# Loading keys and queries of two batches as 128 long runs instead of 96-row pieces

## The chip, the cores and the metric

The kernel runs on one core of a Trainium2 chip. Its time is the device time of one execution in microseconds (us). A core has a matrix engine (TensorE, in the profile PE for its matmuls and PEld for its weight loads), a vector engine (VectorE, DVE), a scalar engine (ScalarE, ACT), GpSimd (POOL) and SyncE (SP), which here does nothing but issue the DMAs of the kernel, one after the other, in one queue. Sixteen DMA engines carry them out.

## The reference

Everything is float32. With q, k, v of shape [8 batches, 8 heads, 576 tokens, 64] and p of [8, 8, 32, 64]:

```python
p_packed = sm_attn(p, k, v)                # 32 packed rows attend to the 576 tokens
out = sm_attn(q, p_packed, p_packed)       # each token attends to the 32 packed rows
x = out.transpose(0, 2, 1, 3).reshape(4608, 512)
h = x @ w_in;  x = (h * sigmoid(h)) @ w_out          # 512 -> 2048 -> 512
h = x @ w_in2; return (h * cos(h)) @ w_out2          # 512 -> 2048 -> 512
```

Here sm_attn(q, k, v) is softmax(q k^T / 8) v. The weights come in as 64-bit words and are decoded to float32 on the core.

## The kernel before

**Phases.** The long part is two stretches of dense matmuls: `first` (lines 985 to 1042) is the first MLP, in 16 steps of 128 hidden columns for each stretch of tokens, and `second` (1211) is the second MLP, in blocks of 256 positions. Ahead of `first` lies the attention. Batches 0 and 1 are done at the very start by the class `Boot` (line 755); batches 2 to 7 are done beside `first` by the class `Steady`, which loads in another way and isn't touched here.

**The order of the work.** Nothing is emitted in program order. Every instruction is recorded in a plan (`Plan`, line 80) with a price in ns (`price`, 163) and what it depends on; a list scheduler (`schedule`, 310) with due times (`DUE`, 469) simulates the engines and the DMA queue by these prices, several times from both ends, and the order that comes out of it is the static order of each engine's instructions and of SP's queue. A DMA's price is its bytes by a rate in GB/s (line 193). A copy may go to ACT or DVE, as the scheduler sees fit (`copy`, 573). Where the plan leaves PE idle between 6 and 60 us, the kernel puts small matmuls on the identity there (`busy`, 1246, called at 429), whose results nobody reads.

**Batches 0 and 1.** `Boot.load` (770) brings a tensor of one batch into one tile `bx` (three of them: k, v, q) by four DMAs of two heads each: 96 partitions, each with a run of six tokens of 64 numbers (1536 bytes) for each head. So partition r holds the tokens 6r to 6r+5 of every head. `turned` (785) transposes pairs of tokens, [96 x 128] to [128 x 96], three for a head, into a PSUM bank, and copies the 288 columns to a tile `bkt`: the even tokens of a pair in the lower 64 partitions, the odd ones in the upper. It does this for the four heads of one group g (0 or 1) at a time, into two of four `bkt` tiles that k and q share.

`stage1` (823) is the attention of p to k: `scores` (806) from `bkt` and the transposed p (`pbd`), the maxima and a copy of the scores to `ba` (834), exponentials, transposes of `ba` in six chunks of 96 (to `bat`). `weighted` (854) multiplies by v: chunk c of the scores must hold the tokens that lie at one place of v's six in all 96 partitions (`values`, 800). Its result is `ppf`. `products` (934) multiplies `ppf` by the first weights. `stage2` (887) turns q, takes the scores against `ppf`, and makes the softmax in the tile `a2`, which `first` reads. Batch 1 uses the same tiles as batch 0, so its loads wait until batch 0 has read them; `change` at line 1307 gives the room of all `Boot` tiles to later weights, once both batches are done.

**Order of tokens.** The columns of `a2` for batches 0 and 1 are not in the order of tokens but as the transposes left them, and stay so through both MLPs. `output` (1135) undoes it: each piece of a block's 128 result rows that lies in one run of 96 positions is written by one DMA, with a step of 6 rows in the output (1143 to 1150). For the other batches the step is 1.

Of the kernel before, what the change touches and what calls it, by code (L numbers as in the profile page):

```python
# [12 lines left out]
F32 = mybir.dt.float32  # L13
F32R = mybir.dt.float32r
I32 = mybir.dt.int32
# [64 lines left out]
class Plan:  # L80
# [4 lines left out]
    PE, DVE, ACT, POOL, DMA, NONE = "PE", "DVE", "ACT", "POOL", "DMA", "NONE"  # L85
# [77 lines left out]
    def price(self, engine, f, out, ins):  # L163

        n = math.prod(out.shape[1:])
        m = max([math.prod(x.shape[1:]) for x in ins], default=n)
        sbuf = all(not str(x.space).endswith("PSUM") for x in ins)
        strided = 44 if ins and n >= 96 and ins[0].ap[-1][0] == 2 else 110 if n >= 96 and out.ap[-1][0] > 2 else 0
        if engine == self.PE:
            if f == "transpose":  # L170
                return 3 + n / 1.2, 0

            if ins[0].dtype == F32R:
                return n / 2.4 + (18 if n == 512 else 7 if n == 256 else 13), 0
            rows, k = out.shape[0], ins[0].shape[0]
            if rows == 128:
                return n * 3.33 + 10, 0
            if rows == 64:
                return n * 0.82, 0
            return {64: 30 if k == 96 else 37, 288: 65, 512: 117}[n], 0  # L180
        if engine == self.DVE:
            if f == "transpose":
                return (67 if sbuf else 160) + (100 if n == 128 else 0) + n / 0.92, 0
            fast = sbuf and f in ("tensor_copy", "tensor_scalar", "memset") and m == n
            if f == "scalar_tensor_tensor" and sbuf and ins[0].dtype == F32:
                return 67 + n / 0.53, 0
            return 67 + max(max(m, n) / (1.92 if fast else 0.96), 60 if f == "reciprocal" else 0) + strided, 0
        if engine == self.ACT:
            return (94 if sbuf else 51) + max(m, n) / 1.2 + (190 if f == "accumulate" else 0) + (105 if f == "sin" else 0) + strided, 0
        if engine == self.POOL:  # L190
            return 149 + (1.7 if any(0 in [st for st, _ in x.ap] for x in ins) else 2.1) * n, 0
        run = min(map(self.contiguous, (out, *ins)))
        return self.ISSUE, 4 * math.prod(out.shape) / (232 if out.dtype == I32 else 260 if run >= 128 else 150)

    @staticmethod
    def contiguous(x):
# [239 lines left out]
def attention_mlps_kernel(  # L436
# [13 lines left out]
    B, H, S, D = q.shape  # L450
# [3 lines left out]
    P = 128  # L454
    HALF = S // 2
# [11 lines left out]
    plan = Plan(nc)  # L467
# [4 lines left out]
    V, A, T, G, DMA = plan.V, plan.A, plan.T, plan.G, plan.D  # L472
# [16 lines left out]
    bpool = boot_stack.enter_context(pool("boot", "right"))  # L489
# [10 lines left out]
    def tiles(pl, shape, dtype, name, n):  # L500

        ts = [pl.tile(shape, dtype, name=f"{name}{i}") for i in range(n)]
        cells.setdefault(pl, []).extend(t.tensor.name for t in ts)
        return ts


    def place(g, h2):
        return (g + h2) % 2
# [14 lines left out]
    STEP = 64  # L523
# [19 lines left out]
    rows = {s: flat(f"m{s}", WIDTH) for s in (1, 2)}  # L543
# [18 lines left out]
    ident = const.tile([P, P], F32, name="ident")  # L562
# [10 lines left out]
    def copy(dst, src):  # L573
        with plan.either():
            A.copy(dst, src)
            V.tensor_copy(dst, src)
# [119 lines left out]
    def cut(t, shape):  # L696
        t = t[:, : math.prod(shape[1:])]
        return t if len(shape) == 2 else t.rearrange("p (a b) -> p a b", a=shape[1])

    CH = 96  # L700
    NCH = S // CH

    class Steady:

        @staticmethod
        def spot(h2, hf):
            return 64 * (h2 ^ hf), HALF * hf

        def __init__(self):
            self.kins = ring(tiles(att, [P, NB, 32], F32, "kin", 2))  # L710
            self.vins = ring(tiles(att, [P, 4 * len(self.chunks), D], F32, "vin", 2))
            self.bigs = ring(tiles(att, [P, S], F32, "big", 3))
            self.a1ts = ring(tiles(att, [P, len(self.chunks) * P], F32, "a1t", 2))
# [41 lines left out]
    class Boot:  # L755

        @staticmethod
        def spot(h2, hf):
            return 64 * hf, HALF * h2

        chunks = [slice(c, c + CH) for c in range(0, S, CH)]

        def __init__(self):
            self.x = dict(zip("kvq", tiles(bpool, [P, H, NCH, D], F32, "bx", 3)))
            self.kt = tiles(bpool, [P, S], F32, "bkt", 4)
            self.a = tiles(bpool, [P, S], F32, "ba", 2)
            self.at = tiles(bpool, [P, NCH * P], F32, "bat", 2)
            self.pp = tiles(bpool, [P, P], F32, "bpp", 2)

        def load(self, n, src, b):  # L770
            plan.unit = ("load", n, b)
            for g in range(2):
                for j in range(2):
                    h = slice(4 * g + 2 * j, 4 * g + 2 * j + 2)
                    DMA.dma_start(
                        self.x[n][:CH, h].rearrange("r h c d -> r h (c d)"),
                        src[b, h].rearrange("h (r c) d -> r h (c d)", c=NCH),
                    )

        def get(self, name, shape, g, j=0):  # L780
            if name == "a1":
                return self.a[g]
            return cut({"kt": self.kt[2 * g + j], "s": self.a[g], "pp": self.pp[g]}.get(name, self.at[g]), shape)

        def turned(self, src, b, g, bank):
            x = self.x["k" if src is k else "q"]
            ts = []
            for j in range(2):
                t = self.get("kt", [P, S], g, j)
                for h2 in range(2):  # L790
                    st = bank()
                    with plan.together():
                        for m in range(3):
                            pair = x[:CH, 4 * g + 2 * j + h2, 2 * m : 2 * m + 2, :].rearrange("r c d -> r (c d)")
                            T.transpose(st[:, m * CH : (m + 1) * CH], pair, ident[:CH, :CH])
                    copy(t[:, h2 * HALF : (h2 + 1) * HALF], st[:, :HALF])
                ts.append(t)
            return ts

        def values(self, b, g):  # L800
            return lambda c, h2, j: self.x["v"][:CH, 4 * g + 2 * j + h2, 2 * (c % 3) + c // 3, :]

    ppf = {}
    a2 = {}
# [18 lines left out]
    def stage1(b, g, bank, mem):  # L823
        plan.unit = ("stage1", b, g)

        plan.margin = plan.SPARE if b >= 2 else 0
        chunks = mem.chunks
        kt = mem.turned(k, b, g, bank)
        a1 = mem.get("a1", [P, S], g)
        mx = maxes()  # L830
        sts = scores(g, pbds[b % 2][:, 2 * g : 2 * g + 2], lambda h2: h2, kt, bank, mem.spot)
        for hf, st in enumerate(sts):
            V.tensor_reduce(mx[:, hf : hf + 1], st, axis=AX.X, op=ALU.max)
            copy(a1[:, hf * HALF : (hf + 1) * HALF], st)
        m = ms()
        V.tensor_scalar(m, mx[:, 0:1], mx[:, 1:2], -SCALE, op0=ALU.max, op1=ALU.mult)
        sums = sumss()
        A.activation(a1[:, :S], a1[:, :S], AF.Exp, bias=m, scale=SCALE, accum_out=sums)
        rs = rss()
        V.tensor_scalar(rs, sums, 1e-9, None, op0=ALU.add)  # L840
        V.reciprocal(rs, rs)
        n = len(chunks)
        lens = [len(range(S)[c]) for c in chunks]
        a1t = mem.get("a1t", [P, n, P], g)
        for c0, c1 in ((0, 4), (4, n)):
            st = bank()
            r = lens[c0]
            for c in range(c0, c1):
                T.transpose(st[:r, (c - c0) * P : (c - c0 + 1) * P], a1[:, chunks[c]], ident)
            copy(a1t[:r, c0:c1, :], st[:r, : (c1 - c0) * P].rearrange("p (c n) -> p c n", n=P))  # L850
        plan.margin = 0
        return lens, a1t, mem.values(b, g), rs
# [282 lines left out]
    def output(i, t):  # L1135

        o = oring()
        if t % 2:
            V.tensor_scalar(o, acc[t], WEIGHT**-2, None, op0=ALU.mult)
        else:  # L1140
            A.activation(o, acc[t], AF.Copy, scale=WEIGHT**-2)
        p0 = order[i] * TB + t % 2 * P
        cuts = [p0] + [c for c in range(p0 + 1, p0 + P) if c % (CH if c <= S else HALF) == 0] + [p0 + P]
        for a, b in zip(cuts, cuts[1:]):
            n, m = divmod(a, HALF)
            if n < 2:
                r0, step = n * S + m % CH * NCH + m // CH * 2 + t // 2, NCH
            else:
                r0, step = n * S + t // 2 * HALF + m, 1
            DMA.dma_start(out[r0 : r0 + (b - a - 1) * step + 1 : step, :], o[a - p0 : b - p0])  # L1150

    gt, st, m5s = {}, {}, {}

# [241 lines left out]
```

## Time and profile before

| | |
|---|---|
| time, median of 3 runs | 1477.23 us (1475.91 to 1480.18) |
| the profiled execution's own time | 1478.51 us |
| its span | 1476.7 us |
| instructions | 34030 |
| ACT busy | 761.9 us (52%) |
| bytes moved by DMA | 296.52 MB, 201 GB/s over the span |

The span is the time from the first to the last instruction that the profile has; some 1.8 us lie around it. Busy time of an engine is the sum of its instructions; matmuls are pipelined, so a busy PE may still be a PE that runs short of its best. The identity matmuls that fill gaps count as busy too.

### The profile page before, as it was taken

The numbers are of one execution on the slowest core, as the hardware profiler recorded it, in microseconds if no ns is written. First come the engines' busy times: TensorE is split into PE (matmuls) and PEld (weight loads), VectorE is DVE, ScalarE is ACT, GpSimd is POOL, SyncE is SP. The second block draws the span as 40 slices with busy tenths as digits, with TensorE's granted clock in tenths as the row PEclk, the third lists the DMA queues.
The fourth block names the chain that finished last, engine by engine and source line by source line (L and its number), as shares of the span: only waits on it lengthen the run. The fifth ranks groups of instructions, "written<-read, shape, count | busy, mean of one in ns | idle before, by whom it ended". The sixth has DMA issues, their size and how long they took to land.

```text
span 1476.7 us, 34030 instructions
## 1 busy us (share of the span) xinstructions
PE 1465.8 (99%) x13100; PEld 1402.8 (95%) x13100; DVE 1139.9 (77%) x2344; ACT 761.9 (52%) x1571; POOL 0.7 (0%) x6
## 2 busy tenths in 40 slices
PE   8999999999999999999999999999999999999998
PEld 6899888899899998999999999999999999999998
DVE  6998787767887687866487778888787877777765
ACT  6976554545456455555354444454454544444443
POOL 0000000000000000000000000000000000000000
PEclk9999999999999999999999999999999999999999
DMA  9776665876867656354777758777676657575560
GB/s 272 210 243 187 163 169 128 242 206 153 215 178 205 208 150 192 129 188 167 268 263 227 228 185 255 230 237 237 214 222 201 215 180 240 182 233 184 191 197 36
DMA packets 313985, 296.52 MB, mean 201 GB/s; under 512 B 172512, under 2 KB 218080, under 8 KB 313824
## 3 DMA queue, kind: packets, MB, share of 16 engines
q1 hardware_dynamic: 313824, 294.35, 66.1%
q8 instruction: 103, 1.69, 0.5%
q14 instruction: 58, 0.48, 0.1%
HBM read 242.81 MB, written 51.45 MB: 199 GB/s over the span
## 4 chain that ended last, share of the span: by engine, by line
PE 96%; DVE 2%; ACT 1%; DMA 0%; issue 0%; SPq 0%; DVEq 0%; ACTq 0%
PE acc L213 54%; PE hb L213 24%; PE mb L213 9%; PE sb L213 9%; DVE rsb L213 0%; ACT ba L213 0%; DMA bx<-in_k 0%; DMA kin<-in_k 0%; DVE ba L213 0%; DVE big L213 0%; ACT bkt L213 0%; DVE wy L213 0%; DVE mx L213 0%; DVE r L213 0%; DVE a L213 0%
## 5 line engine op out<-in xcount | busy, mean ns | idle before, releaser
L213 PE MATMUL acc<-g,w 128*128 128x256 f32 (+2 forms) x3072 | 470.1, 295 | 0.0
L213 PEld LDWEIGHTS acc<-g,w 128*128 128x128 f32 x3072 | 424.7, 188 | 23.4 <-issue 20.5
L213 PE MATMUL acc<-w,g 128*128 128x256 f32 x3456 | 426.7, 276 | 0.0
L213 PEld LDWEIGHTS acc<-w,g 128*128 128x128 f32 x3456 | 408.0, 188 | 0.0
L213 ACT ACTIVATE gf<-hb 128x320 f32<-128x320 f32 (+2 forms) x208 | 95.8, 467 | 103.7 <-PE hb L213 83.4
L213 ACT CAST g<-gf 128x320 fp32r<-128x320 f32 (+2 forms) x194 | 94.4, 488 | 106.1 <-PE acc L213 77.8
L213 DVE TENSOR_TENSOR g<-gf,g 128x320 fp32r<-128x320 f32 (+2 forms) x208 | 108.4, 523 | 46.0 <-PE acc L213 34.2
L213 DVE SCALAR_TENSOR_TENSOR gf<-gf,hb 128x320 f32<-128x320 f32 (+2 forms) x208 | 106.8, 518 | 45.6 <-ACT gf L213 44.4
L213 PE MATMUL hb<-a,w 128*128 128x320 f32 (+2 forms) x768 | 139.9, 298 | 0.6 <-DVE a L213 0.3
L213 PE MATMUL hb<-a,m 128*128 128x320 f32 (+2 forms) x768 | 129.0, 295 | 0.0
L213 ACT ACTIVATE r<-r,half_pi 128x512 f32<-128x512 f32 x144 | 103.7, 720 | 36.9 <-DVE r L213 36.8
L213 ACT CAST g<-r 128x512 fp32r<-128x512 f32 x144 | 89.6, 622 | 61.9 <-DVE r L213 61.7
L213 PEld LDWEIGHTS hb<-a,w 128*128 128x128 f32 x768 | 112.1, 188 | 9.8 <-issue 6.1
L213 PEld LDWEIGHTS hb<-a,m 128*128 128x128 f32 x768 | 109.5, 188 | 7.4 <-issue 5.7
L213 DVE TENSOR_TENSOR g<-r,g 128x512 fp32r<-128x512 f32 x144 | 99.3, 690 | 15.9 <-ACT g L213 15.6
L213 PE MATMUL hb<-w,m 128*128 128x256 f32 x768 | 110.8, 276 | 0.0
L213 DVE SCALAR_TENSOR_TENSOR r<-n,r 128x512 f32<-128x512 int32 x144 | 99.2, 689 | 2.2
L213 ACT ACTIVATE n<-hb 128x512 int32<-128x512 f32 x72 | 43.3, 602 | 108.4 <-PE hb L213 96.5
L213 PEld LDWEIGHTS hb<-w,m 128*128 128x128 f32 x768 | 97.9, 188 | 0.2 <-DVE mb L213 0.2
L213 DVE TENSOR_TENSOR hb<-hb,gf 128x256 f32<-128x256 f32 x72 | 31.1, 432 | 58.0 <-PE hb L213 58.0
L213 ACT ACTIVATE n<-mb 128x512 int32<-128x512 f32 x36 | 21.6, 601 | 82.2 <-PE mb L213 82.1
L213 DVE TENSOR_SCALAR r<-r 128x512 f32<-128x512 f32 x144 | 61.2, 425 | 2.6
(212 smaller groups left out, 1990.7 us busy)
## 6 DMA issues: line engine op xcount, KB each, us to landing
m<-w2s SPq DMA_DIRECT2D x504, 256.0 KB, 3.7
w<-w1dram SPq DMA_DIRECT2D x96, 256.0 KB, 3.7
w2s<-wd SPq DMA_DIRECT2D x28, 512.0 KB, 3.3
wd<-in_moe_w_in SPq DMA_DIRECT2D x24, 512.0 KB, 4.9
wd<-in_moe_w_out SPq DMA_DIRECT2D x20, 512.0 KB, 4.4
raw<-ydram SPq DMA_DIRECT2D x72, 128.0 KB, 3.9
w2dram<-wd SPq DMA_DIRECT2D x16, 512.0 KB, 3.0
w<-w2dram SPq DMA_DIRECT2D x16, 512.0 KB, 5.5
```

The source lines that it names most:

```text
L213: run = lambda: emit(*[real(x) for x in args], **{k: real(x) for k, x in kw.items()})
```

## The change

Keys and queries of batches 0 and 1 are loaded with all 128 partitions: partition 16h + r holds the tokens 36r to 36r + 35 of head h, 9216 bytes in one piece of DRAM, fetched by two DMAs of 4608 bytes for each partition. A transpose now turns two tokens of all eight heads at once, 18 of [128 x 128] for a tensor instead of 24 of [96 x 128]; they are done for both groups when group 0 is due, with five copies of up to 512 columns. k and q have a tile each for the turned form. v is loaded as before. Since v's order of tokens stays, the copy of the scores to `ba` puts them in v's order, with a step of six elements (`place`). The results of batches 0 and 1 are written in runs of 16 positions with a step of 36 rows.

The plan's rates change too: 300 instead of 232 GB/s for integer tiles, and 340 for runs of at least 1024 elements. The entry for 256 columns is a price for small float32 matmuls.

```diff
-            return {64: 30 if k == 96 else 37, 288: 65, 512: 117}[n], 0
+            return {256: 60, 64: 30 if k == 96 else 37, 288: 65, 512: 117}[n], 0
...
-        return self.ISSUE, 4 * math.prod(out.shape) / (232 if out.dtype == I32 else 260 if run >= 128 else 150)
+        return self.ISSUE, 4 * math.prod(out.shape) / (300 if out.dtype == I32 else 340 if run >= 1024 else 260 if run >= 128 else 150)
...
+        RUN = 16
+        STEP = S // RUN
...
-            self.x = dict(zip("kvq", tiles(bpool, [P, H, NCH, D], F32, "bx", 3)))
-            self.kt = tiles(bpool, [P, S], F32, "bkt", 4)
+            self.x = dict(zip("kq", tiles(bpool, [P, self.STEP, D], F32, "bx", 2)))
+            self.v = tiles(bpool, [P, H, NCH, D], F32, "bv", 1)[0]
+            self.kt = dict(zip("kq", tiles(bpool, [P, H, HALF], F32, "bkt", 2)))
...
+            rows = src[b].rearrange("h (r c) d -> (h r) (c d)", c=self.STEP)
+            for c0, c1 in ((0, self.STEP // 2), (self.STEP // 2, self.STEP)):
+                DMA.dma_start(self.x[n][:, c0:c1].rearrange("p c d -> p (c d)"), rows[:, c0 * D : c1 * D])
...
+            for m0 in range(0, self.STEP // 2, 4) if g == 0 else ():
+                m1 = min(m0 + 4, self.STEP // 2)
+                st = bank()
+                with plan.together():
+                    for m in range(m0, m1):
+                        T.transpose(st[:, (m - m0) * P : (m - m0 + 1) * P], self.x[n][:, 2 * m : 2 * m + 2].rearrange("p c d -> p (c d)"), ident)
+                copy(
+                    t[:, :, self.RUN * m0 : self.RUN * m1].rearrange("p h (m r) -> p m h r", r=self.RUN),
+                    st[:, : (m1 - m0) * P].rearrange("p (m h r) -> p m h r", m=m1 - m0, h=H),
+                )
+            return [t[:, 4 * g + 2 * j : 4 * g + 2 * j + 2].rearrange("p h n -> p (h n)") for j in range(2)]
+
+        def place(self, a, st):
+            copy(
+                a.rearrange("p (w r u) -> p u w r", w=NCH // 2, r=self.RUN),
+                st.rearrange("p (u w r) -> p u w r", w=NCH // 2, r=self.RUN),
+            )
...
-            copy(a1[:, hf * HALF : (hf + 1) * HALF], st)
+            mem.place(a1[:, hf * HALF : (hf + 1) * HALF], st)
...
-        cuts = [p0] + [c for c in range(p0 + 1, p0 + P) if c % (CH if c <= S else HALF) == 0] + [p0 + P]
+        run, step = boot.RUN, boot.STEP
+        cuts = [p0] + [c for c in range(p0 + 1, p0 + P) if c % (run if c <= S else HALF) == 0] + [p0 + P]
...
-                r0, step = n * S + m % CH * NCH + m // CH * 2 + t // 2, NCH
+                r0, by = n * S + m % run * step + m // run * 2 + t // 2, step
```

## Rows read from the trace of the kernel before

**Rows 1.** The page: busy us, share and count of engines.
```profile
PE 1465.8 (99%) x13100; PEld 1402.8 (95%) x13100; DVE 1139.9 (77%) x2344; ACT 761.9 (52%) x1571; POOL 0.7 (0%) x6
```

**Rows 2.** Busy time in stretches: stretch, length, busy (count) by engine, clock, DMA, GB/s.
```profile
5.00:10.00 5.00, 5.00 (x41) 4.39 (x39) 2.10 (x8) 2.55 (x7) 0.00 (x0) 1.00 1.04 337
10.00:15.00 5.00, 4.78 (x54) 3.67 (x47) 4.16 (x12) 4.41 (x12) 0.00 (x0) 1.00 1.05 322
15.00:20.00 5.00, 4.45 (x79) 4.16 (x79) 4.63 (x11) 2.82 (x6) 0.00 (x0) 1.00 1.09 270
20.00:25.00 5.00, 4.76 (x81) 3.38 (x81) 2.67 (x5) 2.87 (x7) 0.00 (x0) 1.00 1.08 286
25.00:30.00 5.00, 4.87 (x55) 2.88 (x53) 3.00 (x8) 3.44 (x10) 0.00 (x0) 1.00 1.06 275
...
100.00:120.00 20.00, 20.00 (x160) 18.98 (x159) 20.00 (x43) 15.65 (x37) 0.00 (x0) 1.00 0.76 237
```

**Rows 3.** The same view, the first 66 us in one stretch.
```profile
0.00:66.00 66.00, 59.43 (x705) 48.42 (x706) 52.33 (x142) 50.59 (x124) 0.70 (x6) 1.00 0.89 244
```

**Rows 4.** The chain that ended last, first 140 us: start, us, what.
```profile
0.73 3.14 DMA bx<-in_k
...
61.62 0.48 DVE ba L213
...
65.29 0.44 ACT a L213
...
94.50 5.66 PE acc L213 x43
```

**Rows 5.** Timeline: start, us, engine, line, operation, result<-operands, count, idle before.
```profile
4.01 1.19 PE L213 MATMUL acc<-ident,bx 96*128 96x96 f32 x6 [4.01 <-DMA bx<-in_k]
...
9.34 0.81 PE L213 MATMUL acc<-bkt,pbd 64*32 64x288 f32 x16
...
15.56 2.34 PE L1248 MATMUL acc<-ident 128*128 128x64 f32 x20
...
17.83 0.88 PE L213 MATMUL acc<-bx,bat 96*32 96x64 f32 x48
...
22.78 0.88 PE L213 MATMUL acc<-bx,bat 96*32 96x64 f32 x48
...
26.63 0.45 PE L213 MATMUL hb<-bkt,ppf 64*32 64x288 f32 x4
...
30.51 0.78 PE L213 MATMUL hb<-bkt,ppf 64*32 64x288 f32 x7
...
34.08 0.53 PE L213 MATMUL hb<-a,w 128*128 128x288 f32 x2
```

**Rows 6.** DMA packets between 18 and 22 us.
```profile
DMA packets 766, 1.11 MB, mean 276 GB/s; under 512 B 56, under 2 KB 765, under 8 KB 765
```

**Rows 7.** DMA packets between 8 and 10 us.
```profile
DMA packets 233, 0.83 MB, mean 416 GB/s; under 512 B 30, under 2 KB 30, under 8 KB 233
```

**Rows 8.** DMA issues of the first 60 us: count, KB each, median us to landing.
```profile
bx<-in_q SPq DMA_DIRECT2D x8, 288.0 KB, 11.0
```

**Rows 9.** Groups by form, first 66 us: count, busy us, mean ns, idle before.
```profile
L1248 PE MATMUL acc<-ident 128*128 128x64 f32 x106 | 14.2, 274 | 0.0
...
L213 ACT ACTIVATE wde<-wde 128x512 int32<-128x512 uint32 x11 | 7.6, 694 | 0.0
...
L213 ACT COPY bkt<-acc 128x288 f32<-128x288 f32 x12 | 4.8, 403 | 5.8 <-PE acc L213 5.5
...
L213 ACT COPY bat<-sb 96x512 f32<-96x512 f32 x2 | 1.2, 582 | 0.3 <-PE sb L213 0.2
...
L213 ACT COPY bat<-mb 96x256 f32<-96x256 f32 x2 | 0.7, 372 | 0.0
```

**Rows 10.** DMAs that write the output: issue ns (min/median/max), first and last start.
```profile
L213 SPq DMA_DIRECT2D out<-o x54: 332/413/1203, 824.1 to 1473.7; - x54
```

**Rows 11.** Waits of SP's queue after 700 us: total us, times, longest.
```profile
SPq L213 <- PE hb L213: 308.4, 177, 4.1
```

More of the change, by code (lines that the diff above doesn't have):

```diff
@@ L707, in spot, with place @@
             return 64 * (h2 ^ hf), HALF * hf
+        @staticmethod
+        def place(a, st):
+            copy(a, st)
         def __init__(self):
@@ L771, in load @@
             plan.unit = ("load", n, b)
-            for g in range(2):
-                for j in range(2):
-                    h = slice(4 * g + 2 * j, 4 * g + 2 * j + 2)
+            if n == "v":
+                for h in range(0, H, 2):
                     DMA.dma_start(
-                        self.x[n][:CH, h].rearrange("r h c d -> r h (c d)"),
-                        src[b, h].rearrange("h (r c) d -> r h (c d)", c=NCH),
-                    )
+                        self.v[:CH, h : h + 2].rearrange("r h c d -> r h (c d)"),
+                        src[b, h : h + 2].rearrange("h (r c) d -> r h (c d)", c=NCH),
+                    )
+                return
+            rows = src[b].rearrange("h (r c) d -> (h r) (c d)", c=self.STEP)
+            for c0, c1 in ((0, self.STEP // 2), (self.STEP // 2, self.STEP)):
+                DMA.dma_start(self.x[n][:, c0:c1].rearrange("p c d -> p (c d)"), rows[:, c0 * D : c1 * D])
         def get(self, name, shape, g, j=0):
@@ L782, in get @@
                 return self.a[g]
-            return cut({"kt": self.kt[2 * g + j], "s": self.a[g], "pp": self.pp[g]}.get(name, self.at[g]), shape)
+            return cut({"s": self.a[g], "pp": self.pp[g]}.get(name, self.at[g]), shape)
         def turned(self, src, b, g, bank):
[L786 to L798, printed above, removed]
+            n = "k" if src is k else "q"
+            t = self.kt[n]
+            for m0 in range(0, self.STEP // 2, 4) if g == 0 else ():
[14 more added lines that the diff above has]
+            )
         def values(self, b, g):
-            return lambda c, h2, j: self.x["v"][:CH, 4 * g + 2 * j + h2, 2 * (c % 3) + c // 3, :]
+            return lambda c, h2, j: self.v[:CH, 4 * g + 2 * j + h2, 2 * (c % 3) + c // 3, :]
     ppf = {}
@@ L1146, in output @@
             if n < 2:
-                r0, step = n * S + m % CH * NCH + m // CH * 2 + t // 2, NCH
+                r0, by = n * S + m % run * step + m // run * 2 + t // 2, step
             else:
-                r0, step = n * S + t // 2 * HALF + m, 1
-            DMA.dma_start(out[r0 : r0 + (b - a - 1) * step + 1 : step, :], o[a - p0 : b - p0])
+                r0, by = n * S + t // 2 * HALF + m, 1
+            DMA.dma_start(out[r0 : r0 + (b - a - 1) * by + 1 : by, :], o[a - p0 : b - p0])
     gt, st, m5s = {}, {}, {}
```

## The prediction

> **What bounds the kernel now.** I read the page first. PE is busy for 1465.8 of 1476.7 us [rows 1]: over the whole there is almost no idle time to win, so the question is where a busy PE does useless or thin work. The busy times by stretch answer it. Between 100 and 120 us PE gets through 160 matmuls in 20 us, one in 125 ns, without idle time [rows 2]; that is the dense state, and it lasts to the end. The first 66 us are different: PE counts as busy for 59.4 us [rows 3], but 14.2 us of that are 106 identity matmuls put into gaps [rows 9], and much else is small attention work. The change can pay only by bringing forward the moment from which PE is dense, or by thinning out what precedes it.
>
> The chain of waits shows that moment. It runs over PE, ACT and DVE pieces of batch 0 and 1, and the last part that isn't PE goes from 61.62 us (DVE, batch 1's second softmax) to the ACT cast of `a` that ends at 65.73; after it the chain stays on PE, as in the piece of 43 matmuls at 94.5 us [rows 4]. So I take 66 us as the end of the start-up, and what ends it is softmax and decoding on DVE and ACT, not a DMA.
>
> Two resources are short ahead of that. The DMA engines are full: their share is 1.04 to 1.09 in each 5 us stretch from 5 to 30 us [rows 2], and the issues of q take 11.0 us at the median to land, since they stand behind others [rows 8]. DVE has idle time only early: 2.90, 0.84, 0.37, 2.33 and 2.00 us in the five stretches from 5 to 30 us, 8.4 in all [rows 2]. Over 66 us it is busy for 52.3 [rows 3], and of the 13.7 idle us 8.4 are those and up to 5 lie in the first 5 us, so from 30 us on DVE is as good as full. Work that DVE gets earlier, in place of these 8.4 us, moves everything behind it.
>
> The timeline says what DVE waits for between 20 and 30 us. The second product with v runs at 22.78 us, the scores of q for group 0 at 26.63 and for group 1 at 30.51, the first matmul of the MLP at 34.08 [rows 5]. The scores need `ppf` and q. Twenty identity matmuls stand ahead of the first product with v, from 15.56 to 17.90 us [rows 5]: the plan expected to wait here.
>
> **The change part by part.**
>
> Transfers. One tensor of one batch has 8 x 576 x 64 x 4 = 1.18 MB. From 18 to 22 us nearly all packets lie between 512 bytes and 2 KB, which are the 1536-byte runs of k, q and v: 276 GB/s [rows 6], so 4.27 us for a tensor. From 8 to 10 us, 203 of 233 packets lie between 2 and 8 KB, the rows of the weights (512 KB on 128 partitions, so 4096 bytes): 416 GB/s [rows 7], so 2.84 us. In both stretches the engines are full, so this is the price by length. No row has a run of 4608 bytes; the nearest is 4096, and I take its rate: 1.43 us saved for each of four tensors. The low end is the rate of before, saving nothing; above 416 I don't go. What counts for batch 0 is when q has landed. Ahead of that lie its k, itself, and about half of batch 1's k, which the queue puts in between: 2.5 tensors, 3.6 us. k comes first of all, when little queues behind it and the first wait is mostly its own flight (issued at 0.73, first transposes at 4.01 [rows 4, 5]), so I count half of its part: 2.9 us, with ends 0 and 3.6.
>
> The Trainium skill has a rule against this term: its page "DMA: Bandwidth & Descriptors", section "Specifications", gives 512 bytes as the least transfer for line rate, so that runs of 1536 bytes would be at full rate already. The trace disagrees, 276 against 416 GB/s [rows 6, 7]; by the rule this term would be 0 and the sum 0.6 us.
>
> The first step. Transposes of group 0 now need a part of every head, and both halves of k instead of its first two DMAs. Against that the scores of group 0 run only at 9.34 us though its transposes began at 4.01 [rows 5], and those of group 1 no longer trail. I price it at 0, between half a microsecond gained and 0.7 lost (the 295 KB more that must land, at 416 GB/s).
>
> Copies of turned tiles. Before: 8 for a tensor at 403 ns, 3.22 us. After: four of 512 columns at 582 and one of 256 at 372, 2.70 us [rows 9]. That is 0.52 us for each of four tensors, 2.1 in all. They are reordered on the way out, in runs of 16 elements, which no row shows; I use the plain price.
>
> The reordering copies of scores. Eight copies of 288 columns (two batches, two groups, two halves) now write with a step of six elements. No row has that step. The nearest is the ACT operation on every second element, 694 ns for 512 where a plain copy takes 582 [rows 9]: 0.22 ns an element, 0.06 us for 288. At the other end I double the copy, 0.40 more. I take 0.1, so 0.8 us in all, between 0 and 3.2. The Trainium skill ("SBUF — State Buffer", section "Door 1: The DMA port swizzle") says that each access that crosses to another 16-byte line of SBUF pays a penalty, which a step of 24 bytes does every time; no run here shows it, and it gives no duration for these engines.
>
> Copies and reordering together take 1.3 us off ACT and DVE. Half of it I put on the path: 0.6 us, with ends -1.0 (the doubled copies) and 1.3.
>
> Transposes on PE: 72 of 128 columns for 96 of 96 columns, the same columns all told, in stretches where PE has fillers. Nothing; if that cover were gone, still nothing.
>
> Tiles. k and q no longer share the turned tile, and batch 1's k may be fetched as soon as 18 transposes are done. This helps the same wait as the transfers and isn't counted again.
>
> Output. The 576 positions of batches 0 and 1, for both halves of the tokens, were 18 of the 54 DMAs [rows 10]; in runs of 16 they are 72. The 54 more cost SP 54 x 0.413 = 22 us [rows 10] in three blocks of the second MLP, 7.4 us a block, six or so more issues behind each of four results. Queued behind them on SP are the loads of weights for the coming steps. SP waits 308 us in that phase for PE to release buffers of such loads [rows 11], so it is ahead of need; a buffer ring of 16 with 7 loads a step of about 10.5 us (the kernel's due times) gives some 24 us. So 0; without that cover PE would lose up to 7.4 us a block.
>
> The planner. It now expects the weights, k and q earlier, so fewer identity matmuls and earlier places for what depends on them. I count that with the transfers, as the condition that their 2.9 us are used, not as a term.
>
> Sum: 2.9 + 0.6 = 3.5 us. It must fit into DVE's idle time between 20 and 30 us, which is 4.3 us, and it does. The profiled execution took 1478.5 us and would take 1475.0; it lies 1.3 above the median of 1477.2, so for the median I say 1473.7.
>
> **The rivals.**
>
> First: the transfers aren't the wait, or runs of 4608 bytes are served no faster than those of 1536. For it: in the chain DMA appears only with the first 3.14 us [rows 4], and its DVE work from 30 us on is the same. Against it: DVE's 4.3 idle us at 20 to 30 while q is on its way. Then the copies alone are left, -0.6: 1476.6, between 1475.5 and 1478.5.
>
> Second: the whole early idle time goes. If earlier data and fewer fillers let the decoding fill also 5 to 20 us, all 8.4 us of DVE's idle time would be open. For it: the fillers at 15.56. Against it: 2.9 of the 8.4 lie at 5 to 10 us, where DVE has its first input only then. 1477.2 - 7 = 1470.
>
> Third, the other side: batch 1 becomes the later one. Its chain ends the start-up at 65.7 us, with 4.1 us on DVE and ACT on it [rows 4]. Now its group 0 needs the transposes and copies of all heads through two banks, between other work on a full DVE; the new order may put that stretch later by as much again as it is long, and more where the weights that inherit the tiles wait for it. It decides when batch 1's second softmax ends later than at 65.7 us. 4.1 us lost and little won: 1481.
>
> **How the numbers follow.** Forecast (2 to 5.5 us gained) 0.50, first rival 0.23, second 0.15, third 0.12. About 0.3%, 4.4 us, is what a measurement here can tell from no change: under 1472.8 counts as faster. Of the forecast's 0.50 I put 0.20 there (its upper part), with the second rival 0.35. Same is 0.30 + 0.23 = 0.53, slower 0.12. The range goes from 1469.5, which leaves out part of the second rival, to 1478.5, where the third begins.
>
> **What would show it.** Right: packets of 2 to 8 KB for k and q at nearly 400 GB/s; scores of q near 23 us for both groups; the first `hb<-a,w` near 31 instead of 34.08; DVE's idle time in 20 to 30 us down from 4.3 to about 1; the last stretch off PE in the chain ending near 62. Wrong: the same times for these with full DMA, or a later end of batch 1's softmax, or a PE idle after 700 us beside rows of `out<-o`.

## The result: slower, though the start-up gained

| | before | changed kernel |
|---|---|---|
| time, median of 6 runs each | 1476.92 us (1475.91 to 1480.18) | 1487.83 us (1484.14 to 1492.24) |
| the profiled execution / its span | 1478.51 / 1476.7 us | 1485.88 / 1484.1 us |

The ratio is 1.0073, 95% interval [1.0058, 1.0088]: 10.9 us slower, where 3.5 us faster was forecast. The profiled execution is one of the shorter ones, 7.4 us above that of before. All readings of it below are to be seen against these 7.4 us.

The page of the changed kernel: engines, then the chain that ended last, by engine and by line.

```profile
PE 1466.6 (99%) x13080; PEld 1401.4 (94%) x13080; DVE 1140.5 (77%) x2350; ACT 757.4 (51%) x1553; POOL 0.7 (0%) x6
...
PE 88%; DMA 5%; DVE 3%; ACT 2%; SPq 1%; issue 1%; ACTq 0%; DVEq 0%
PE acc L213 50%; PE hb L213 22%; PE sb L213 9%; PE mb L213 9%; SPq L213 1%; DMA wd<-in_moe_w_in 1%; DMA ypart<-ysb 1%; DMA ysb<-ypart 1%; DMA w2s<-wd 1%; DMA m<-w2s 1%; DVE r L213 1%; DMA w<-w1dram 0%; DVE big L213 0%; ACT ba L213 0%; DVE w
```

The same line of the chain on the page of before:

```profile
PE 96%; DVE 2%; ACT 1%; DMA 0%; issue 0%; SPq 0%; DVEq 0%; ACTq 0%
```

PE's busy time is as before [rows 1], within 0.8 us; the span is 7.4 us longer, so PE now waits. On the page of before DMA had 0% of the chain; here it has 5%, some 74 us, and none of the names belong to the tensors that were changed: decoded weights, partial sums, weights of the second MLP, all later work.

**The start-up.** Busy times by stretch, in the same columns as [rows 2, 3]:

```profile
5.00:10.00 5.00, 5.00 (x26) 5.00 (x24) 2.10 (x8) 2.36 (x5) 0.00 (x0) 1.00 1.03 309
10.00:15.00 5.00, 4.69 (x62) 3.78 (x61) 3.93 (x10) 4.48 (x9) 0.00 (x0) 1.00 1.08 260
15.00:20.00 5.00, 4.14 (x118) 3.04 (x118) 3.66 (x12) 4.32 (x11) 0.00 (x0) 1.00 1.02 393
20.00:25.00 5.00, 5.00 (x48) 3.98 (x42) 3.41 (x6) 3.77 (x7) 0.00 (x0) 1.00 1.03 410
25.00:30.00 5.00, 4.84 (x62) 2.88 (x56) 3.27 (x8) 3.46 (x9) 0.00 (x0) 1.00 1.06 291
...
100.00:120.00 20.00, 20.00 (x160) 19.00 (x159) 19.73 (x42) 16.07 (x38) 0.00 (x0) 1.00 0.58 203
```

The packets between 18 and 22 us, which answer to [rows 6]:

```profile
DMA packets 405, 1.64 MB, mean 411 GB/s; under 512 B 45, under 2 KB 45, under 8 KB 405
```

The new loads reach what the sum took from the rows of before: 411 GB/s where 276 was, with full engines. But the timeline of PE shows that batch 0 got little of it:

```profile
4.57 1.97 PE L213 MATMUL acc<-ident,bx 128*128 128x128 f32 x8 [2.42 <-DMA bx<-in_k]
...
10.41 1.21 PE L213 MATMUL acc<-bkt,pbd 64*32 64x288 f32 x32 [0.19 <-ACT bkt L213]
...
17.11 1.55 PE L213 MATMUL acc<-bv,bat 96*32 96x64 f32 x96
...
26.66 0.45 PE L213 MATMUL acc<-bkt,ppf 64*32 64x288 f32 x4 [0.15 <-ACT bkt L213]
...
28.33 0.45 PE L213 MATMUL hb<-bkt,ppf 64*32 64x288 f32 x4
...
34.74 0.53 PE L213 MATMUL hb<-a,w 128*128 128x288 f32 x2 [0.30 <-ACT a L213]
```

Against [rows 5]: the first transposes 0.56 us later (more of k must land), the products with v of both groups done by 18.7 us where the second began at 22.78, the scores of q at 26.66 for the first group, as before, and at 28.33 instead of 30.51 for the other, and the first matmul of the MLP 0.66 us later. The landing times in the two traces tell a part of why the first group gained nothing. The whole q of batch 0 landed at 22.4 us, where it was 25.7; but the half that group 0 needed had landed at 21.3 before, and now its scores wait until all eight heads are turned.

Batch 1 isn't earlier either. In the chain of before its second softmax stood from 61.62 to 65.73 us [rows 4], and here the last piece of such work in the chain ends at 43.1:

```profile
42.90 0.22 ACT ba L213
...
61.75 5.27 PE acc L213 x40
```

That is a change of the chain and not of the work. The last of the four casts of `a` for batch 1 starts at 74.23 us, where it was 73.00, and before the change PE was busy for all but 0.08 us of that stretch. The casts, before and changed, and PE's busy time in the stretch before the change:

```profile
73.00 0.43 ACT L213 CAST a<-bat 128x288 fp32r<-128x288 f32 x1
```

```profile
74.23 0.44 ACT L213 CAST a<-bat 128x288 fp32r<-128x288 f32 x1
```

```profile
61.62:65.78 4.16, 4.08 (x31) 3.85 (x31) 4.10 (x14) 4.16 (x11) 0.00 (x0) 1.00 0.77 199
```

What the start-up gained is small: PE comes to its first products `mb<-w,ppf` at 78.07 us, where it was 78.84. Some expectations below speak of 2.5 to 3.4 us up to 169 us; from 80 us on the two kernels do their work in different orders, and such a lead isn't the start-up's.

Copies by form, in the columns of [rows 9]: one line of before, then two of the changed kernel. The turned tiles cost what was said (588 ns); the reordering copies of scores took 722 ns where the plain ones of before took 412, 0.3 us more each, not 0.1:

```profile
L213 ACT COPY ba<-acc 128x288 f32<-128x288 f32 x4 | 1.4, 412 | 0.0
```

```profile
L213 ACT COPY bkt<-acc 128x512 f32<-128x512 f32 x6 | 3.5, 588 | 5.4 <-PE acc L213 5.4
...
L213 ACT COPY ba<-acc 128x288 f32<-128x288 f32 x4 | 2.3, 722 | 0.0
```

**Where the time goes.** PE's busy time in three stretches, the kernel before and then the changed one:

```profile
240.00:290.00 50.00, 50.00 (x404) 43.19 (x403) 42.41 (x84) 26.49 (x54) 0.00 (x0) 1.00 0.76 208
370.00:425.00 55.00, 55.00 (x421) 48.62 (x420) 43.78 (x92) 27.43 (x59) 0.00 (x0) 1.00 0.77 205
1000.00:1300.00 300.00, 300.00 (x2645) 300.00 (x2644) 237.13 (x490) 143.84 (x279) 0.00 (x0) 1.00 0.66 210
```

```profile
240.00:290.00 50.00, 48.46 (x387) 41.26 (x386) 37.57 (x71) 22.04 (x48) 0.00 (x0) 1.00 0.70 171
370.00:425.00 55.00, 53.76 (x486) 46.82 (x492) 41.61 (x83) 22.85 (x52) 0.00 (x0) 1.00 0.72 191
1000.00:1300.00 300.00, 298.84 (x2628) 298.43 (x2627) 237.88 (x493) 143.50 (x277) 0.00 (x0) 1.00 0.67 211
```

PE was never idle there before; now it is short by 1.5, 1.2 and 1.2 us, and from 165 to 425 us by 5.0 in all. Of the 7.4 us, 6.3 are lost by the first result of the second MLP and 0.9 from there to the last one (the lines stand in experiment 7). One such wait can be followed. First SP's queue in the changed kernel, then ACT:

```profile
262.63 6.41 SPq L213 DMA_DIRECT2D kin<-in_k  x13
269.14 2.08 SPq L213 DMA_DIRECT2D w<-w1dram  x4
271.27 1.43 SPq L213 DMA_DIRECT2D kin<-in_k  x3
272.74 0.93 SPq L213 DMA_DIRECT2D wd<-in_moe_w_in  x2
```

```profile
268.98 0.68 ACT L213 CAST a<-big 128x576 fp32r<-128x576 f32 x1 [0.17 <-DVE big L213]
277.23 0.67 ACT L213 ACTIVATE wd<-wd 128x512 int32<-128x512 uint32 x1 [7.57 <-DMA wd<-in_moe_w_in]
```

SP issues sixteen small loads of a later batch's keys, each 0.5 us of its time, ahead of a load of weights that starts only at 272.74 and lands at 277.2. ACT's next instruction in its fixed order is the decoding of these weights, so ACT stands for 7.57 us; behind it stand the tanh of the hidden columns, DVE, and PE. No engine is full here: from 240 to 290 us ACT is busy for 22.0 of 50 us, and the share of the DMA engines is 0.70. The load is late because of its place in SP's queue.

The last group of the changed kernel, for [rows 10, 11]: 108 output DMAs for 54, at the same issue time each.

```profile
L213 SPq DMA_DIRECT2D out<-o x108: 314/417/1479, 830.4 to 1480.9; - x108
```

### The profile page after: what moved, and what is told of

The parts are those of the page before. It is cut to its first block, busy times and chain, and to the rows that moved or that the text cites. A ratio compares the mean times of both kernels' runs of the same rounds, so it can differ in the third digit from the quotient of the medians.

```text
span 1484.1 us, 34048 instructions
## 1 busy us (share of the span) xinstructions
PE 1466.6 (99%) x13080; PEld 1401.4 (94%) x13080; DVE 1140.5 (77%) x2350; ACT 757.4 (51%) x1553; POOL 0.7 (0%) x6
## 4 chain that ended last, share of the span: by engine, by line
PE 88%; DMA 5%; DVE 3%; ACT 2%; SPq 1%; issue 1%; ACTq 0%; DVEq 0%
PE acc L213 50%; PE hb L213 22%; PE sb L213 9%; PE mb L213 9%; SPq L213 1%; DMA wd<-in_moe_w_in 1%; DMA ypart<-ysb 1%; DMA ysb<-ypart 1%; DMA w2s<-wd 1%; DMA m<-w2s 1%; DVE r L213 1%; DMA w<-w1dram 0%; DVE big L213 0%; ACT ba L213 0%; DVE w L213 0%
## 5 line engine op out<-in xcount | busy, mean ns | idle before, releaser
L213 DVE TENSOR_TENSOR g<-r,g 128x512 fp32r<-128x512 f32 x144 | 99.0, 688 | 16.3 <-ACT g L213 16.0
```

The lines of the kernel that those rows point to most:

```text
L213: run = lambda: emit(*[real(x) for x in args], **{k: real(x) for k, x in kw.items()})
```

## The experiments

Three theories. **A**: the new rates make the plan order the later loads too tightly. **B**: the layout costs it (output DMAs, order of tokens). **C**: the list scheduler answers to any small change of its input with another order of all later work, some of them worse by several us; the change only dealt the cards again. Ratios are to runs of the kernel before on the same chip.

**1. layout_old_rates.** The change with the old rates.

```diff
-(300 if out.dtype == I32 else 340 if run >= 1024 else 260 if run >= 128 else 150)
+(232 if out.dtype == I32 else 260 if run >= 128 else 150)
```

> The whole change, but the plan's DMA rates as before (232 GB/s for integer tiles, 260 for long runs). Theory A (the new rates make the plan order the later loads and stores too tightly, which costs some 10 us between 165 and 425 us and after): the loss goes, the gain of 2.5 to 3.4 us seen up to 169 us stays, 1473 to 1476 us. Theory B (the layout itself costs it: the 54 more output DMAs, the order of tokens): still 1484 to 1490. Theory C (the list scheduler answers to any small change of its input by some us either way, whatever the change means): anything from 1470 to 1490, and the place of the loss moves.

Measured: 1483.67 against 1477.21 us, 1.0046 [1.0033, 1.0059]. Against A in its simple form: the loss is smaller but there. B's range is missed as well, by 0.3 us. Of the 4.9 us between the profiled executions 1.8 are lost ahead of the first result of the second MLP and 3.0 behind it, where the output DMAs are.

**2. before_new_rates.** The same edit the other way, in the kernel before.

> The kernel before with nothing but the two new DMA rates in the plan. Theory A: 1483 to 1490 us, with waits of PE between 165 and 425 us as in the changed kernel, and no gain in the start-up, or 1 us. Theory B: 1477 +- 2. Theory C: anything from 1470 to 1490.

Measured: 1486.88 us, 1.0066 [1.0052, 1.0079]. The loss of the changed kernel without any of its layout, so B isn't needed for it. It fits A or C.

**3. before_cut16.**

```diff
-c % (CH if c <= S else HALF) == 0
+c % (16 if c <= S else HALF) == 0
```

> The kernel before with the output of batches 0 and 1 cut at every 16 positions instead of 96: 72 DMAs for 18, same bytes and same rows. Theory A: 1477 to 1479 us, at most the 1.2 us by which PE was short between 1000 and 1300 us in the changed kernel. Theory B: 1480 or more. Theory C: these DMAs come last in the plan, so little, 1475 to 1480.

Measured: 1479.84 us, 1.0017 [1.0008, 1.0025]. Above A's range, just under B's, inside C's. B's own cost is 2.6 us by this run, with some change of the order in it.

**4. before_nudge and before_nudge2.** 234, then 230, for 232 GB/s.

> The kernel before with one rate of the plan changed by under a hundredth (234 for 232 GB/s): a change that means nothing to the hardware. Theory A: 1476 to 1479 us. Theory B: the same. Theory C: off by 3 us or more, either way, with the order of SP's queue changed all over.

> The kernel before with 230 for 232 GB/s, the other side of the first nudge. If the kernel before sits at an order that was picked for its time: slower by 2 to 6 us, as with 234. If the first nudge was bad luck: within 1.5 us of 1477, or faster.

Measured: 1481.78 against 1477.21 us, 1.0029 [1.0019, 1.0040]; and 1480.08 against 1479.44, 1.0003 [0.9990, 1.0015]. A rate that differs by less than a hundredth costs 4.6 us in one direction and nothing in the other. That is C: another order of almost the same instructions (with 234, four filler matmuls fewer, and five operations on ACT instead of DVE) is worth that much. It doesn't show that the kernel before was at the best order.

**5. after_nudge.** 302 for 300 GB/s in the changed kernel.

> The changed kernel with one rate of the plan changed by under a hundredth (302 for 300 GB/s). Theory C: off from the changed kernel's 1487.8 by 3 us or more, either way, most likely downwards, 1478 to 1486, with the waits of PE at other places. Theory B: 1486 to 1490.

Measured: 1489.58 us, 1.0068 [1.0056, 1.0081]; my guess of a move downwards was wrong, and so was C's of 3 us or more: it is 1.8 us above the changed kernel.

**6. after_i32_old and after_340_old.** One of the two rates put back.

> The changed kernel with the old rate for integer tiles (232), the new one for long runs (340). If the rate of 300 is what puts the weights' loads too close to their decoding: 1479 to 1485, and PE busy for 49.5 to 50 of the 50 us from 240 to 290 us, where the three kernels with 300 or 302 have 46.6 to 48.5. If any order is as bad as any other: 1480 to 1490, with no relation to that stretch.

> The changed kernel with 300 for integer tiles, and the old 260 for long runs. By the rate of 300: 1485 to 1490, and PE short by 1.5 us or more from 240 to 290 us. If any order is as bad as any other: 1480 to 1490.

Measured: 1484.74 us, 1.0036 [1.0022, 1.0049], with 232; 1479.06 us, 0.9994 [0.9983, 1.0006], with 260. The first met its expectation (PE busy for 49.63 of the 50 us from 240 us). My expectation for the second failed: with 300 kept, the loss is gone, and PE is busy for all of the 50 us. So the rate of 300 alone isn't what costs. The rate of 340 alone costs 5 us, both together 11, neither (run 1) 6. As times, such numbers don't add up as costs of edits do; they look like draws of an order.

The traces say more. The sum of ACT's waits for the loads of weights from 165 to 425 us (us, times, longest), in the kernel before, with 300 alone, with 340 alone, and in the changed kernel:

```profile
ACT wd L213 <- DMA wd<-in_moe_w_in: 3.9, 2, 2.0
```

```profile
ACT wd L213 <- DMA wd<-in_moe_w_in: 7.6, 4, 2.7
```

```profile
ACT wd L213 <- DMA wd<-in_moe_w_in: 10.2, 5, 3.0
```

```profile
ACT wd L213 <- DMA wd<-in_moe_w_in: 16.3, 5, 7.6
```

These waits go with the rates and not with the layout: 3.0 to 3.9 us in the five kernels with the old rates or a rate within a hundredth of one (before, runs 1, 3 and 4), 12.6 to 16.3 in the three with both new rates (changed, runs 2 and 5). Those three are 9.7 to 11.2 us slower than the kernel before, and none of the other six orders of the scheduler by more than 6.5. So A isn't refuted. A plan that counts on faster loads seems to ask for them too late, and the wait of 7.57 us followed above is of that kind. How much of the loss this makes, beside C, no run separates.

**7. hybrid75, hybrid160 and reverse75.** To keep the instructions and change only the order, the plan's start times and its choice between ACT and DVE were read from a table: up to the seam (75 or 160 us) those of the kernel itself, from there on those that the other kernel's plan gave to the same operation.

```diff
     def order(self):
-        (the list scheduler, rounds from both ends)
+        self.start = START          # from a table: own plan up to the seam, the other's after it
+        for i, o in enumerate(self.ops):
+            if o.choice: o.engine = ON_DVE[i]
+            for j in o.after:
+                self.start[i] = max(self.start[i], self.start[j])
+        return sorted(range(n), key=lambda i: (self.start[i], i))
```

> The changed kernel, all of its instructions, but from 75 us of the plan on the static order (and the choice of ACT or DVE for copies) is that of the kernel before; ahead of 75 us it is the changed kernel's own. Theory C (the loss is the new order of the later work, the layout itself gains what the start-up shows): 1473 to 1477 us, the gain of 1 to 3 us of the first 80 us kept, no PE waits between 165 and 425 us. Theory B (the layout costs it: output DMAs, transfers): 1483 or more.

> The same with the seam at 160 us of the plan: the changed kernel's own order up to there, where its trace was 2.5 to 3.4 us ahead. Theory C: 1473 to 1476 us. Theory B: 1483 or more.

> The kernel before, all of its instructions, but from 75 us of the plan on in the changed kernel's order. Theory C: it loses what the changed kernel lost after 165 us, some 10 us, so 1484 to 1489. Theory B: 1477 to 1479.

Measured: hybrid75 1484.73 us against 1478.40, 1.0036 [1.0023, 1.0049]; hybrid160 1494.28, 1.0105 [1.0090, 1.0121]; reverse75 1500.75, 1.0145 [1.0129, 1.0162]. The last two say little: both lose several us right behind their seam (from 75 to 170 us PE is busy for 92.19 and 86.56 of 95 us), where two orders that don't fit meet. hybrid75 missed its number too, but its trace splits the question; from 78 us on its PE runs the matmuls in the order of the kernel before, but for a few places. The copies of results of the second MLP, their first and last start, in the kernel before, the changed kernel and hybrid75:

```profile
L213 ACT ACTIVATE o<-acc x18: 600/600/604, 823.5 to 1472.3; 128x512 f32<-128x512 f32 x18
```

```profile
L213 ACT ACTIVATE o<-acc x18: 600/600/600, 829.8 to 1479.5; 128x512 f32<-128x512 f32 x18
```

```profile
L320 ACT ACTIVATE o<-acc x18: 592/598/598, 820.4 to 1477.7; 128x512 f32<-128x512 f32 x18
```

With the order of before, the changed kernel is 3.1 us ahead at 820 us; in its own order it is 6.3 us behind at the same result. So the order of the work between 75 and 820 us, with the choice of ACT or DVE in it, is worth 9.4 us, by one execution of each.

The start-up gave only a part of the 3.1 us. The same matmuls in the kernel before and in hybrid75:

```profile
78.84 0.63 PE L213 MATMUL mb<-w,ppf 64*32 64x512 f32 x4
...
261.47 0.56 PE L213 MATMUL acc<-g,w 128*128 128x320 f32 x2
```

```profile
78.26 0.63 PE L320 MATMUL mb<-w,ppf 64*32 64x512 f32 x4
...
260.05 0.56 PE L320 MATMUL acc<-g,w 128*128 128x320 f32 x2
```

hybrid75 is 0.6 us ahead at 78 us, 1.4 at 260, where weight loads on PE waited 1.5 us for `w` in the kernel before and 0.5 in hybrid75, and 2.6 at 390. The kernels of experiment 8 are 1.4 to 1.6 us ahead at 78 us. Whether other executions of the kernel before also lose time at 260 and 390 us isn't known: there is one trace of it.

After the first result hybrid75 falls back by 8.5. Its one long wait of PE after 1000 us, and SP's queue ahead of it:

```profile
1082.35 1.65 PE L320 MATMUL hb<-w,m 128*128 128x256 f32 x6 [5.99 <-DVE mb L320]
```

```profile
1066.35 3.59 SPq L320 DMA_DIRECT2D out<-o  x8
1070.04 0.37 SPq L320 DMA_DIRECT2D m<-w2s  x1
1070.50 2.72 SPq L320 DMA_DIRECT2D out<-o  x6
1073.32 1.63 SPq L320 DMA_DIRECT2D m<-w2s  x1
1075.05 2.70 SPq L320 DMA_DIRECT2D out<-o  x6
1077.80 0.90 SPq L320 DMA_DIRECT2D ysb<-ypart  x2
```

Twenty output DMAs stand ahead of a load of partial sums for the next block (`ysb<-ypart`); DVE's addition waits for that load (6.9 us), and PE for DVE. Here it is B's mechanism, by the small loads for the next block in the same queue and not by loads of weights. The wait of 6.0 us costs more than itself, since the granted clock behind it is 0.50 for 4.7 us:

```profile
1082.35:1087.00 4.65, 4.65 (x22) 4.65 (x23) 1.73 (x4) 1.26 (x3) 0.00 (x0) 0.50 0.69 223
```

At half the clock these 4.65 us do the work of some 2.3. With the wait that makes 8.3 of the 8.5 us, by this estimate.

**8. hybrid75_spread, hybrid75_slow, hybrid75_out18.** The seam as in hybrid75; the 8 output DMAs of a result 2.4 us apart, then 8 us apart, then cut as in the kernel before (which puts the rows of batches 0 and 1 at other places of the output: the new order of the output is left out).

```diff
-start of an output DMA: that of its result
+start of the k-th output DMA: that of its result + 1.3 us + 2.4 us * k      (spread)
+start of the k-th output DMA: that of its result + 6 us + 8 us * k          (slow)
...
-        run, step = boot.RUN, boot.STEP
+        run, step = CH, NCH                                                  (out18)
```

> As hybrid75, whose blocks stay 2.6 to 3.1 us ahead of the kernel before up to 820 us and which then loses 6 us at one PE wait at 1082 us, behind 20 output DMAs in a row on SP's queue. Here the 54 more output DMAs are spread in the order, 2.4 us apart, behind the loads that the next block waits for. If the order of the later work is the whole loss: 1473.5 to 1475.5 us, no PE wait over 1 us between 1000 and 1300 us. If the output DMAs cost SP's time however they are placed: 1477 to 1485, with PE waits at 1080 us and one and two blocks later.

> As hybrid75_spread, a full kernel, with the 8 output DMAs of a result 8 us apart, so that SP is never held for more than some 0.5 us on their account. If the place of the output DMAs in SP's queue is what costs: 2 to 3 us faster than the kernel before. If their number costs however they are placed: still a PE wait of 2 us or more behind a load between 1000 and 1300 us, and the same time as the kernel before or slower.

> As hybrid75, but the output of batches 0 and 1 is written as in the kernel before, in runs of 96 positions with a step of 6 rows, so those rows land at other places of the output (left out: the new order of the output). Loads, transposes and reordering copies are the changed kernel's, the later order and the number of output DMAs those of the kernel before. If order and output DMAs are the whole loss: 2.5 to 3.5 us faster than the kernel before, with no PE wait over 1 us after 66 us. If the layout costs something else: same or slower.

Measured: spread 1480.86 against 1479.44 us, 1.0013 [1.0002, 1.0024], still with a PE wait of 2.9 us at 1093 us, so 2.4 us apart was not enough; slow 1474.81 against 1477.87, 0.9985 [0.9976, 0.9995]; out18 1474.95 against 1477.87, 0.9985 [0.9976, 0.9994]. The copies of results and two stretches of hybrid75_slow:

```profile
L320 ACT ACTIVATE o<-acc x18: 598/598/600, 819.5 to 1469.9; 128x512 f32<-128x512 f32 x18
```

```profile
240.00:290.00 50.00, 50.00 (x420) 44.66 (x420) 43.96 (x86) 26.96 (x56) 0.00 (x0) 1.00 0.75 209
1000.00:1300.00 300.00, 298.53 (x2624) 298.14 (x2623) 235.32 (x485) 142.96 (x276) 0.00 (x0) 1.00 0.65 208
```

With the old order behind the seam, and with output DMAs that are few or far apart, the change is worth 2.9 to 3.1 us (0.7 to 3.5 by the intervals). hybrid75_slow is a full kernel and beats both the kernel before and the changed one. PE is still short by 1.5 us from 1000 to 1300 us in it, where out18 is short by 0.2.

## Why the prediction was wrong

Its direction and range were wrong, and the step that failed is the one that has no term: "The planner. [...] I count that with the transfers, as the condition that their 2.9 us are used, not as a term." Every instruction of this kernel takes its place from a list scheduler, and the edit changed the scheduler's prices and its first tasks. The new order is the largest number of the case: 9.4 us between hybrid75 and the changed kernel at the first result. The nine other kernels whose order is the scheduler's own (the changed one and runs 1 to 6) lie from -0.4 to +11 us. ACT's waits for loads of weights, which go with the rates, grow from 3.9 to 16.3 us in the changed one. The rows of before couldn't give the size, but they could have given a warning: PE is busy for 99% of the span [rows 1], and DVE for 99.15 of the 100 us from 30 to 130, so the order has little slack. That another order is then more likely worse is an argument, not a measurement; none of the other scheduler's orders beat it clearly.

The sum itself was too large as well. Its 3.5 us were to come at the start-up, and there, at 78 us, the traces show 0.8 us in the changed kernel and 0.6 to 1.8 in hybrid160, hybrid75 and the three kernels of experiment 8. Two readings behind it failed. It counted from the landing of the whole q, but group 0's scores had needed only half of it; the whole q came 3.3 us sooner, and those scores came no sooner. And it took the chain's 4.1 us off PE before 65.73 us for the end of the start-up; PE was busy for 4.08 of 4.16 us there, and the cast that ends at 65.73 is the first of four for batch 1.

"Output. [...] So 0" failed too, though little of this loss is due to it. The count (54 more, 0.41 us each) was right; the cover was not, since I checked only the loads of weights. The small loads for the next block go through the same queue and are needed sooner. From the first result to the last the kernel before takes 648.8 us; the changed kernel takes 0.9 more, hybrid75_slow 1.6, run 1 3.0 and hybrid75 8.5, by the place of the DMAs. before_cut16 puts them at 2.6.

The third rival had the sign (slower) and not the mechanism: batch 1's second softmax did end later, by 1.2 us at its last cast, but the chain doesn't pass through it, and the loss lies after 165 us.

What held: the rates of the transfers (411 GB/s for the 416 assumed, 276 before), and the whole q landed 3.3 us sooner for the 2.9 counted. But "the price by length" isn't shown to be one by length. In the trace of before, packets of 1152 bytes took 51 ns at the median (66 to 425 us), those of 4096 bytes 159, and the 1536-byte ones of the first 66 us 98, with the shortest at 65: more for a byte than either. So these traces don't refute the Trainium skill's 512 bytes for line rate ("DMA: Bandwidth & Descriptors", section "Specifications"), as the prediction took the 276 GB/s to do. The 1536-byte runs also go to 96 partitions, the long ones to 128; no run separates that from length.

What held in sum only: hybrid75_slow and out18 are 2.9 to 3.1 us faster than the kernel before, near the 3.5 of the sum, but at most 1.6 of it is there at 78 us, and the rest comes later at places that the prediction didn't name. That the sums agree is in part luck. The places: the scores of q came at 26.7 and 28.3 us, not 23, and DVE's idle time from 20 to 30 us fell from 4.3 to 3.3 us, not to 1.

The copies: I counted 1.3 us off ACT and DVE, but the reordering ones cost 0.3 us more each, 2.5 in all, which eats the 2.0 us that the turned tiles save (5 x 588 ns or less for 8 x 403). That was inside the bounds given, at their far end. The Trainium skill's rule on crossing 16-byte lines ("SBUF — State Buffer", section "Door 1: The DMA port swizzle") fits that row, but no run separates it from another cause.

Open: which property of an order makes it good. The runs show the places where the bad ones wait (a load of weights behind small loads, ACT behind that load), not a rule by which the scheduler would have seen it. Open too is how the changed kernel's loss divides between the rates and the chance of another order.

## What to carry to other kernels

Where a scheduler places every instruction, an edit has two effects, its own and a new order of everything; measure them apart, by holding the order fixed or by nudging a price that means nothing, before an edit is judged by its time. A nudge by under a hundredth moved this kernel by 4.6 us, more than the edit is worth. Times alone looked like chance here; the waits for one kind of load, summed in each trace, showed that those waits went with the rates. And when DMAs are added to a queue, look at every load that shares it and is needed soon, not only at the largest.

## What the runs showed of the hardware that was not expected

A copy on ACT from PSUM to SBUF of 288 columns takes 412 ns with plain writes and 722 ns with a step of 24 bytes, runs of one element.

A long wait in dense work can cost more than its own length. In hybrid75 PE was idle for 6.0 us ahead of 1082.35 us; the granted clock was then 0.50, so 1.2 instead of 2.4 GHz, up to 1087 us, and 0.98 from 1087 to 1091. In reverse75 PE waited once for 7.6 us behind ACT, and the granted clock from 75 to 170 us is 0.93 on the mean, so about a seventh of that stretch was at 1.2 GHz; in the kernel before it is 1.00 there.
